# Two weight conversions and the decay table early on ScalarE's queue, a later split of the first block's sums, and 768 of 1024 weight columns split

## The chip, the cores and the metric

The kernel runs on one core of a Trainium2 chip. The metric is the device time of one execution in microseconds. The engines of the core are TensorE (PE in the profile; PEld is its weight load), VectorE (DVE), ScalarE (ACT), GpSimd (POOL) and SyncE (SP); SP and ACT issue the transfers here, each on a queue of its own.

## What is computed

The reference is a retention layer followed by two feed-forward layers, all in float32:

```
for each block of 64 positions:                       # q, k, v: 2 x 8 heads x 768 x 64
    intra = (q_b k_b^T * Dmask) v_b                   # Dmask[i,j] = lam^(i-j) for i >= j, else 0
    inter = (q_b * lam^(i+1)) kv_state
    out_b = intra + inter
    kv_state = lam^block * kv_state + (k_b * lam^(block-1-i))^T v_b
x = out as 1536 tokens x 512
g = relu(x @ w_in)^2 ;            x = g @ w_out       # 512 -> 2048 -> 512
h = sigmoid(x @ w_gate) * (x @ w_val) ; y = h @ w_out # 512 -> 1536 -> 512
```

## The kernel before, in words

**Stages.** The kernel takes the sequence in 12 chunks of 128 positions (two batch entries of six chunks each) in the order `ORDER`. The first seven chunks are the lead, ahead of the first feed-forward matmul. The other five are put between the steps of the first layer (`SLOTS`). The 1536 tokens form three blocks of 512. Block 0 goes through layer 1 step by step (`step_1`, 16 steps of 128 hidden columns). Blocks 1 and 2 go through the layer's first matrix together by a scheme that needs seven products for a two by two block product (`strassen`, eight pairs of steps in layer 1), and then through the second matrix (`pair_out`). The second layer does the same with `step_2`, twelve pairs and `pair_out`.

**Precision.** Every float32 operand of the feed-forward matmuls is split into a high part (a ScalarE copy to fp32r) and a low part (a VectorE subtraction), and a product is three matmuls. The loaded weights come in as float64; ScalarE makes two pieces of each 128 x 512 unit (`conv_act`, L150 and L151), VectorE puts them together in three operations (`conv_dve`), and SP stores the unit to DRAM, from where it is loaded again when it is needed. A weight pair is loaded as four 256-column blocks (`load_a`), combined to four sums by VectorE (`combine_a`), and both sets are split (`high_a`, `low_a`). The inputs are combined likewise: T1 to T4 are differences of quarters of blocks 1 and 2 (`combine_x`).

**Lead.** `powers` loads lambda to 128 partitions (8 heads x 16), raises it on POOL, and writes the powers to a small table in DRAM behind a row of zeros and a one. `decays` reads the table D (all partitions, each one element further) and the rows L back from there. For each chunk, `att_scores` needs q and k; `att_prep` lets POOL make kd = k x a column of D and qd = q x L, and VectorE mask the scores with D (L287). `att_out` makes the state update from kd (L314), the output from the masked scores (L322) and, for chunks that are not the first of their batch entry, from qd and the state (L329). `att_state` and `att_x` take the results out of the accumulators. `UP` chunks have their scores ahead of the loop; `LOOP` names the loads that each chunk issues and `CONVS` how many conversions it does. `conv_act` also asks for the next weight unit.

**Order.** The order on each engine is the order of the program. `passed(us)` moves a clock by the time of the matmuls emitted, and `at(pos, fn)` puts work on an agenda that is emitted when the clock has passed its place. `T1` is the start of `strassen` of the first layer, `T2` its end. In `step_1` each step does `PACE[f]` conversions while more than 36 units are left.

**Around T1.** In the first pair of `strassen` the closing product of block 0 (`close(1)`) follows the second of the seven products; `evacuate(1)` then takes its four sums out of PSUM and splits them at once into x0, the input of `step_2`. The products go in the order A11 with B11, S1 with T1, (close), S2 with T2, S4 with B22, S3 with T3, A12 with B21; A22 with T4 comes in the next pair.

Of the kernel before, what the change touches and what calls it, by code (L numbers as in the profile page):

```python
# [12 lines left out]
P = 128  # L13
# [5 lines left out]

ORDER = (0, 6, 1, 2, 7, 3, 8, 4, 9, 5, 10, 11)  # L20
LEAD = 7
UP = 4
SLOTS = ((1, 3), (5, 8), (11, 13), (16, 19), (22, 25))


FIRST = "q0 q1 v0"
SIDE = "q2 q3"
EARLY = "D v1 w q4"
LOOP = ("v2 v3 q5", "q6 v4 v5 w", "v6 w v7", "q7", "", "", "")
RAW_BUFS = 4  # L30

CONVS = (1, 0, 1, 1, 1, 1, 0)
PACE = (2, 2, 2, 2, 2, 2, 2, 2, 2, 2, 2, 2, 2, 2, 1, 0)

MM = 0.2267
# [5 lines left out]
def retention_moe_kernel(  # L41
# [95 lines left out]

    ready = []

    def conv_act():  # L140

        if not to_conv or to_conv[0] not in raw_t:
            return
        key = to_conv.pop(0)
        t = raw_t.pop(key)
        j = unit("j")
        r = unit("r", I32)
        nc.scalar.activation(j, t[:, :, 1].bitcast(F32), AF.Copy, scale=2.0**-112)  # L150
        nc.scalar.activation(r, t[:, :, 0].bitcast(mybir.dt.uint32), AF.Copy, scale=2.0**-29)  # L151
        ready.append((key, j.bitcast(I32), r))
        load_w(1)

    def conv_dve():

# [42 lines left out]
    L = const.tile([P, 4, CH], F32, name="L")  # L199
    S = [const.tile([P, 4, 64], F32, name=f"S{i}", tag=f"S{i}") for i in range(2)]  # L200
    w_dram = dram.tile([H, 256], F32, name="w_dram")

    def powers():


        src = bass.AP(lam.tensor, lam.offset, [[1, H], [0, 16], [1, 1]])
        nc.sync.dma_start(out=lam_sb, in_=src)
        nc.vector.memset(warm, 0.0)
        nc.gpsimd.iota(exi, pattern=[[1, 8]], base=0, channel_multiplier=8)
        nc.vector.memset(Z[:, 0:127], 0.0)  # L210
        nc.vector.memset(Z[:, 127:128], 1.0)
        nc.vector.tensor_scalar(
            out=exi, in0=exi, scalar1=127, scalar2=None, op0=ALU.bitwise_and
        )
        nc.vector.tensor_scalar(out=ex, in0=exi, scalar1=1.0, scalar2=None, op0=ALU.add)
        nc.scalar.dma_start(out=w_dram[:, 0:128], in_=Z)
        nc.gpsimd.tensor_tensor(out=W, in0=lam_sb.to_broadcast([P, 8]), in1=ex, op=ALU.pow)
        dst = w_dram[:]
        nc.scalar.dma_start(
            out=bass.AP(dst.tensor, dst.offset + 128, [[256, H], [8, 16], [1, 8]]), in_=W  # L220
        )

    def decays():


        src = w_dram[:]
        nc.sync.dma_start(
            out=D, in_=bass.AP(src.tensor, src.offset, [[1, P], [256, H], [1, CH]])
        )
        for r in range(2):  # L230
            nc.sync.dma_start(
                out=L[64 * r : 64 * r + 64],
                in_=bass.AP(src.tensor, src.offset + 256 * r + 128, [[0, 64], [512, 4], [1, CH]]),
            )
# [14 lines left out]
    def new_xr():  # L249
        for t in (1, 2):  # L250
            xr[t] = xp.tile([P, 4, TB], F32, tag=f"xr{t}", name=f"xr{t}")
# [17 lines left out]
    def att_prep(c):  # L269
        n = c % SEQ_CH  # L270
        sc = sc_t.pop(c)
        at_t[c] = double("at")
        dst = [pv(at_t[c][:, r, :]) for r in range(2)]
        qt = qk_t.pop(c)[:, 0, :]
        kn = kv_t[c][:, 0, :]
        if n < SEQ_CH - 1:
            kd = kd_t[c] = unit("kd")
            nc.gpsimd.tensor_tensor(  # L278
                out=kd.rearrange("s (h d) -> s h d", h=H),
                in0=kn.rearrange("s (h d) -> s h d", h=H),  # L280
                in1=D[:, :, CH - 1 : CH].to_broadcast([P, H, 64]), op=ALU.mult,
            )
        if n > 0:
            qd = qd_t[c] = unit("qd")
            nc.gpsimd.tensor_tensor(out=pv(qd), in0=pv(qt), in1=L, op=ALU.mult)  # L285
        return [
            lambda r=r: nc.vector.tensor_tensor(  # L287
                out=dst[r], in0=pv(sc[r]), in1=Dv[:, r], op=ALU.mult
            )
            for r in range(2)  # L290
        ]
# [146 lines left out]
    def evacuate(ph):  # L438
        for e, acc in enumerate(accs.pop(ph)):
            if ph == 1:  # L440
                nc.scalar.copy(x0[0][:, e, :], acc)
                nc.vector.tensor_tensor(
                    out=x0[1][:, e, :], in0=acc, in1=x0[0][:, e, :], op=ALU.subtract
                )
            else:
                o = unit("o")
                (nc.scalar.copy if e % 2 == 0 else nc.vector.tensor_copy)(o, acc)
                nc.sync.dma_start(out=out[e, :, 0:TB], in_=o)
# [9 lines left out]
        1: dram.tile([NF1, P, 2, TB], F32, name="g1"),  # L458
        2: dram.tile([NF2, P, 2, TB], F32, name="g2"),
    }  # L460
    A11, A12, A22 = (0, 0), (0, 1), (0, 3)
    S3, S4, S1, S2 = (1, 0), (1, 1), (1, 2), (1, 3)

    def split_x(name, src):
        hi, lo = xc[name] = double("xch", F32R), double("xcl", F32R)
# [42 lines left out]
    def combine_a(key):  # L508
        a = a_t[key]
        s = as_t[key] = wp.tile([P, 4, 256], F32, tag="w", name="as")  # L510
        tt = nc.vector.tensor_tensor
        tt(out=s[:, 0:2], in0=a[:, 0:2], in1=a[:, 2:4], op=ALU.subtract)
        tt(out=s[:, 2], in0=a[:, 2], in1=a[:, 3], op=ALU.add)
        tt(out=s[:, 1], in0=s[:, 0], in1=s[:, 1], op=ALU.add)
        tt(out=s[:, 3], in0=a[:, 3], in1=s[:, 0], op=ALU.subtract)

    def high_a(key, part):
        hi = wp.tile([P, 4, 256], F32R, tag="w", name="ah")
        lo = wp.tile([P, 4, 256], F32R, tag="w", name="al")
        nc.scalar.copy(hi, (a_t, as_t)[part][key])  # L520
        s_t[(*key, part)] = hi, lo

    def low_a(key, part):
        hi, lo = s_t[(*key, part)]
        src = (a_t, as_t)[part].pop(key)
        nc.vector.tensor_tensor(out=lo, in0=src, in1=hi, op=ALU.subtract)  # L526

    def prepare_a(key, pos):
# [93 lines left out]
    def keep_g(ph, f, t, g):  # L622
        held.append(lambda: nc.sync.dma_start(out=g_dram[ph][f, :, t], in_=g))

    def pair_in_1(i):
        def use(di, t, c, in_psum):
            g = unit("g")
            if in_psum:
                r = unit("r")
                nc.scalar.activation(r, c, AF.Relu)  # L630
                nc.vector.scalar_tensor_tensor(
                    out=g, in0=c, scalar=0.0, in1=r, op0=ALU.max, op1=ALU.mult
                )
            elif di == 1:
                r = unit("r")
                nc.scalar.activation(r, c, AF.Relu)
                nc.scalar.activation(g, r, AF.Square)
            else:
                nc.vector.scalar_tensor_tensor(
                    out=g, in0=c, scalar=0.0, in1=c, op0=ALU.max, op1=ALU.mult  # L640
                )
            keep_g(1, 2 * i + di, t, g)

        return [use]

    def pair_in_2(i):
        gate = {}

        def use_gate(di, t, c, in_psum):
            r = gate[di, t] = unit("r")  # L650
            nc.scalar.activation(r, c, AF.Sigmoid)

        def use_val(di, t, c, in_psum):
            g = unit("g")
            nc.vector.tensor_tensor(out=g, in0=c, in1=gate.pop((di, t)), op=ALU.mult)
            keep_g(2, 2 * i + di, t, g)

        return [use_gate, use_val]

# [63 lines left out]
    def load(what, eng=nc.sync):  # L723

        for x in what.split():
            if x == "w":
                load_w(1)
            elif x == "D":
                decays()
            elif x[0] == "q":  # L730
                load_qk(order[int(x[1:])], eng)
            else:
                load_kv(order[int(x[1:])], eng)
# [71 lines left out]
    with tc.manual_schedule():  # L805
        powers()
        load(FIRST)
        load(SIDE, nc.scalar)
        warm_up()
        load(EARLY)  # L810
        new_xr()
        for k in range(UP):
            att_scores(order[k])
        run(att_prep(order[0]))
        for k, c in enumerate(order[:lead]):
            att_out(c)
            if UP <= k + 3 < lead:
                att_scores(order[k + 3])
            load(LOOP[k])
            ops = conv_dve()  # L820
            if k + 1 < lead:
                weave(att_prep(order[k + 1]), ops[:2])
                run(att_state(c))
                att_decay(order[k + 1])
                weave(ops[2:], att_x(c))
            else:
                weave(split_w(1, 0), ops)
                rest.append(c)
            for m in range(CONVS[k]):
                if m:  # L830
                    run(conv_dve())
                conv_act()
            flush()


        keys = [(1, i, 0) for i in range(NF1 // 2)]
        prepare_a(keys[0], T1)
        at(T1 - 20.0, lambda: load_a((1, 1, 0)))
        combine_x([T1 + d for d in (-30, -25, -15, -13, -11, -9, -7, 2, 4, 6, 8)])
        for f in range(NF1):  # L840
            step_1(f)
        n_out = 24
# [93 lines left out]
```

## Time and profile before

| | |
|---|---|
| three runs | 604.19, 600.67, 601.86 us (median 601.86) |
| profiled execution, first to last instruction | 599.4 us (this span is all that is known of its own time) |
| TensorE busy | 582.6 us, 97% |
| VectorE, ScalarE, POOL busy | 448.6, 332.5, 36.9 us |
| DMA | 127.19 MB, mean 212 GB/s |

Busy is the time in which an engine executes; a matmul is counted from its start to its modelled end. The table by stretch gives for each engine the busy time and, in brackets, the number of instructions. A timeline row begins with the start and the duration in us; what stands in square brackets at its end is how long the engine was idle ahead of it and what released it. SPq and ACTq are issues of transfers by SyncE and ScalarE.

### The profile page before, as it was taken

To read this page: it belongs to the slowest core of one execution; us is meant where nothing else is said; L and a number is where in the kernel's file an instruction comes from. 1 tells how busy PE (TensorE), PEld (TensorE's weight loads), DVE (VectorE), ACT (ScalarE), POOL (GpSimd) and SP (SyncE) were. 2 spreads that over 40 slices of the span, in tenths; PEclk is the share of its full clock that TensorE was granted. 3 is DMA by queue.
4 is the path that set the end of the run, shared out by engine and by line. 5 is a ranking of instruction groups with operands and counts; after the bars stand their busy time and mean duration, and the time that the engine had idled before them with its cause. 6 is when DMAs were issued, how large, how long until landed. Compare 5 with 4: busy or idle time off the path is not lost.

```text
span 599.4 us, 8496 instructions
## 1 busy us (share of the span) xinstructions
PE 582.6 (97%) x3076; PEld 478.8 (80%) x3076; DVE 448.6 (75%) x673; ACT 332.5 (55%) x525; POOL 36.9 (6%) x34
## 2 busy tenths in 40 slices
PE   7799999999899999999999999999999999999997
PEld 7677878887678888888888888888888888888885
DVE  0699998999888868988877788694778787569101
ACT  0367787988556456756557654554464455537101
POOL 1672212100000000000000000000000000000000
PEclk9899999999999999999999999999999999999999
DMA  7996898682145377999978945511332422658003
GB/s 212 402 418 232 306 309 331 237 297 87 57 121 208 107 240 271 408 414 415 410 276 279 312 170 172 163 50 54 122 106 106 140 81 80 209 187 357 0 1 141
DMA packets 53578, 127.19 MB, mean 212 GB/s; under 512 B 5784, under 2 KB 7584, under 8 KB 53536
## 3 DMA queue, kind: packets, MB, share of 16 engines
q1 hardware_dynamic: 52376, 124.41, 57.9%
q10 hardware_dynamic: 1160, 2.24, 1.1%
q8 instruction: 24, 0.39, 0.3%
q14 instruction: 18, 0.15, 0.1%
HBM read 90.96 MB, written 35.66 MB: 211 GB/s over the span
## 4 chain that ended last, share of the span: by engine, by line
PE 87%; DVE 4%; DMA 2%; POOL 2%; issue 2%; ACT 1%; SPq 0%; ACTq 0%; POOLq 0%; DVEq 0%
PE p L545 30%; PE p L695 25%; PE p L386 17%; PE p L400 12%; DMA kv<-in_kv 1%; POOL kd L278 1%; PE p L329 1%; PE p L322 1%; POOL qd L285 1%; DMA lam_sb<-in_lam 1%; PE p L264 1%; DVE wlo L374 1%; DVE al L526 1%; DVE m L175 1%; ACT ah L520 1%
## 5 line engine op out<-in xcount | busy, mean ns | idle before, releaser
L545 PE MATMUL p<-xcl,ah 128*128 128x512 f32 x280 | 109.1, 390 | 2.5 <-DVE xcl L469 2.5
L545 PE MATMUL p<-xch,ah 128*128 128x512 f32 x280 | 109.4, 391 | 0.4 <-ACT s L554 0.2
L545 PE MATMUL p<-xch,al 128*128 128x512 f32 x280 | 109.0, 389 | 0.0
L695 PE MATMUL p<-g2h,whi 128*128 128x512 f32 x224 | 87.1, 389 | 0.0
L695 PE MATMUL p<-g2l,whi 128*128 128x512 f32 x224 | 87.1, 389 | 0.0
L695 PE MATMUL p<-g2h,wlo 128*128 128x512 f32 x224 | 87.1, 389 | 0.0
L545 PEld LDWEIGHTS p<-xcl,ah 128*128 128x128 f32 x280 | 52.6, 188 | 13.5 <-DVE xcl L469 2.9
L545 PEld LDWEIGHTS p<-xch,ah 128*128 128x128 f32 x280 | 52.5, 188 | 12.9 <-ACT s L554 1.4
L545 PEld LDWEIGHTS p<-xch,al 128*128 128x128 f32 x280 | 52.6, 188 | 11.0
L559 DVE TENSOR_TENSOR c<-p,s 128x512 f32<-128x512 f32 x60 | 41.2, 688 | 25.3 <-PE p L545 21.4
L554 ACT COPY s<-p 128x512 f32<-128x512 f32 x60 | 35.0, 586 | 37.4 <-PE p L545 37.4
L167 DVE CUSTOM_DVE_ANT_0 u<-m,r 128x1024 uint16<-128x1024 uint16 x68 | 49.5, 728 | 2.7
L374 DVE TENSOR_TENSOR wlo<-u,whi 128x512 fp32r<-128x512 f32 x68 | 46.1, 707 | 7.0 <-ACT whi L372 5.7
L150 ACT ACTIVATE j<-raw 128x512 f32<-128x512 f32 x68 | 45.6, 671 | 10.2 <-issue 5.3
L175 DVE SCALAR_TENSOR_TENSOR m<-j,m 128x512 int32<-128x512 int32 x68 | 49.5, 728 | 1.2
L151 ACT ACTIVATE r<-raw 128x512 int32<-128x512 uint32 x68 | 45.2, 665 | 8.7 <-PE p L695 5.5
L695 PEld LDWEIGHTS p<-g2l,whi 128*128 128x128 f32 x224 | 42.0, 188 | 8.8
L695 PEld LDWEIGHTS p<-g2h,whi 128*128 128x128 f32 x224 | 42.0, 188 | 8.7
L695 PEld LDWEIGHTS p<-g2h,wlo 128*128 128x128 f32 x224 | 42.0, 188 | 8.7
L372 ACT CAST whi<-u 128x512 fp32r<-128x512 f32 x68 | 39.0, 616 | 13.7 <-DVE u L167 13.2
L386 PE MATMUL p<-xh,wlo 128*128 128x512 f32 x160 | 43.2, 392 | 1.1 <-DVE wlo L374 1.1
L386 PE MATMUL p<-xh,whi 128*128 128x512 f32 x160 | 43.8, 395 | 0.0
(87 smaller groups left out, 911.6 us busy)
## 6 DMA issues: line engine op xcount, KB each, us to landing
raw<-in_w SPq DMA_DIRECT2D x68, 512.0 KB, 7.1
w<-u SPq DMA_DIRECT2D x68, 256.0 KB, 4.0
u<-w SPq DMA_DIRECT2D x64, 256.0 KB, 5.5
g<-g SPq DMA_DIRECT2D x56, 256.0 KB, 4.4
g<-g SPq DMA_DIRECT2D x28, 512.0 KB, 7.5
a<-w SPq DMA_DIRECT2D x20, 512.0 KB, 4.3
kv<-in_kv SPq DMA_DIRECT2D x12, 512.0 KB, 8.6
qk<-in_qk SPq DMA_DIRECT2D x10, 512.0 KB, 5.7
```

The source lines that it names most:

```text
L150: nc.scalar.activation(j, t[:, :, 1].bitcast(F32), AF.Copy, scale=2.0**-112)
L151: nc.scalar.activation(r, t[:, :, 0].bitcast(mybir.dt.uint32), AF.Copy, scale=2.0**-29)
L167: nc.vector.tensor_tensor(out=w.bitcast(I32), in0=m, in1=r, op=ALU.add)
L175: lambda: nc.vector.scalar_tensor_tensor(out=m, in0=j, scalar=-(2**31), in1=m, op0=ALU.bitwise_and, op1=ALU.bitwise_or),
L372: nc.scalar.copy(hi, src)
L374: lambda lo=lo, src=src, hi=hi: nc.vector.tensor_tensor(out=lo, in0=src, in1=hi, op=ALU.subtract)
L386: nc.tensor.matmul(acc, lhsT=a[:, kk * P : (kk + 1) * P], rhs=b[:, kk, :], start=i == 0, stop=i == 11,)
L400: nc.tensor.matmul(acc[e], lhsT=a[:, e * P : (e + 1) * P], rhs=b, start=first and i == 0, stop=last and i == 2,)
L545: nc.tensor.matmul(acc, lhsT=w[:, col, kk * P : (kk + 1) * P], rhs=x[:, kk, :], start=start and i == 0, stop=stop and i == 5, skip_group_c ...
L554: nc.scalar.copy(s, acc)
L559: nc.vector.tensor_tensor(out=c, in0=acc, in1=s, op=ALU.add)
L695: nc.tensor.matmul(acc[e, t], lhsT=a[:, e * P : (e + 1) * P], rhs=b[:, t, :], start=first and i == 0, stop=last and i == 2,)
```

## The change

`UP` goes from 4 to 3. All early loads are issued by SP, in the order `FIRST` and `NEXT`, with two weight units behind the first q. ScalarE does the first conversion, then issues D, does the second, and issues L; VectorE finishes both conversions ahead of the loop. Conversions in the lead no longer ask for the next unit; `LOOP` names them. POOL makes the column that kd needs (`KD`) from a second load of lambda (one row of eight heads for each partition), so that kd does not read D. `evacuate(1)` copies the four sums to SBUF and puts their split on the agenda, 20 to 46 us later. The two halves of a weight pair change places, so that the block that no product uses alone (A21) comes first and is left out of the split; the four sums are made by four operations of 256 columns. Four places of `combine_x` are a little earlier.

```diff
@@ -19,17 +19,15 @@
 
 ORDER = (0, 6, 1, 2, 7, 3, 8, 4, 9, 5, 10, 11)
 LEAD = 7
-UP = 4
+UP = 3
 SLOTS = ((1, 3), (5, 8), (11, 13), (16, 19), (22, 25))
 
 
-FIRST = "q0 q1 v0"
-SIDE = "q2 q3"
-EARLY = "D v1 w q4"
-LOOP = ("v2 v3 q5", "q6 v4 v5 w", "v6 w v7", "q7", "", "", "")
-RAW_BUFS = 4
-
-CONVS = (1, 0, 1, 1, 1, 1, 0)
+FIRST = "q0 w w q1 v0 q2 v1"
+NEXT = "q3 v2 q4 v3 w"
+LOOP = ("q5 v4 w", "q6 v5 w", "v6 w", "w q7", "v7 w", "w", "w")
+
+CONVS = (0, 0, 1, 1, 1, 1, 1)
 PACE = (2, 2, 2, 2, 2, 2, 2, 2, 2, 2, 2, 2, 2, 2, 1, 0)
 
 MM = 0.2267
@@ -137,7 +135,7 @@
 
     ready = []
 
-    def conv_act():
+    def conv_act(more=True):
 
 
 
@@ -150,7 +148,8 @@
         nc.scalar.activation(j, t[:, :, 1].bitcast(F32), AF.Copy, scale=2.0**-112)
         nc.scalar.activation(r, t[:, :, 0].bitcast(mybir.dt.uint32), AF.Copy, scale=2.0**-29)
         ready.append((key, j.bitcast(I32), r))
-        load_w(1)
+        if more:
+            load_w(1)
 
     def conv_dve():
 
@@ -199,6 +198,10 @@
     L = const.tile([P, 4, CH], F32, name="L")
     S = [const.tile([P, 4, 64], F32, name=f"S{i}", tag=f"S{i}") for i in range(2)]
     w_dram = dram.tile([H, 256], F32, name="w_dram")
+    lam8 = const.tile([P, H], F32, name="lam8")
+    exk = const.tile([P, 1], I32, name="exk")
+    exf = const.tile([P, 1], F32, name="exf")
+    KD = const.tile([P, H, 1], F32, name="KD")
 
     def powers():
 
@@ -206,6 +209,9 @@
         src = bass.AP(lam.tensor, lam.offset, [[1, H], [0, 16], [1, 1]])
         nc.sync.dma_start(out=lam_sb, in_=src)
         nc.vector.memset(warm, 0.0)
+        src = bass.AP(lam.tensor, lam.offset, [[0, P], [1, H]])
+        nc.scalar.dma_start(out=lam8, in_=src)
+        nc.gpsimd.iota(exk, pattern=[[1, 1]], base=0, channel_multiplier=1)
         nc.gpsimd.iota(exi, pattern=[[1, 8]], base=0, channel_multiplier=8)
         nc.vector.memset(Z[:, 0:127], 0.0)
         nc.vector.memset(Z[:, 127:128], 1.0)
@@ -213,22 +219,30 @@
             out=exi, in0=exi, scalar1=127, scalar2=None, op0=ALU.bitwise_and
         )
         nc.vector.tensor_scalar(out=ex, in0=exi, scalar1=1.0, scalar2=None, op0=ALU.add)
+        nc.vector.tensor_scalar(out=exf, in0=exk, scalar1=0.0, scalar2=None, op0=ALU.add)
         nc.scalar.dma_start(out=w_dram[:, 0:128], in_=Z)
         nc.gpsimd.tensor_tensor(out=W, in0=lam_sb.to_broadcast([P, 8]), in1=ex, op=ALU.pow)
         dst = w_dram[:]
         nc.scalar.dma_start(
             out=bass.AP(dst.tensor, dst.offset + 128, [[256, H], [8, 16], [1, 8]]), in_=W
         )
-
-    def decays():
+        nc.gpsimd.tensor_tensor(
+            out=KD[:, :, 0], in0=lam8, in1=exf.to_broadcast([P, H]), op=ALU.pow
+        )
+        nc.vector.memset(KD[0:1], 1.0)
+
+    def decay_table():
 
 
         src = w_dram[:]
-        nc.sync.dma_start(
+        nc.scalar.dma_start(
             out=D, in_=bass.AP(src.tensor, src.offset, [[1, P], [256, H], [1, CH]])
         )
+
+    def decay_rows():
+        src = w_dram[:]
         for r in range(2):
-            nc.sync.dma_start(
+            nc.scalar.dma_start(
                 out=L[64 * r : 64 * r + 64],
                 in_=bass.AP(src.tensor, src.offset + 256 * r + 128, [[0, 64], [512, 4], [1, CH]]),
             )
@@ -278,7 +292,7 @@
             nc.gpsimd.tensor_tensor(
                 out=kd.rearrange("s (h d) -> s h d", h=H),
                 in0=kn.rearrange("s (h d) -> s h d", h=H),
-                in1=D[:, :, CH - 1 : CH].to_broadcast([P, H, 64]), op=ALU.mult,
+                in1=KD.to_broadcast([P, H, 64]), op=ALU.mult,
             )
         if n > 0:
             qd = qd_t[c] = unit("qd")
@@ -438,9 +452,14 @@
     def evacuate(ph):
         for e, acc in enumerate(accs.pop(ph)):
             if ph == 1:
-                nc.scalar.copy(x0[0][:, e, :], acc)
-                nc.vector.tensor_tensor(
-                    out=x0[1][:, e, :], in0=acc, in1=x0[0][:, e, :], op=ALU.subtract
+                x = unit("xd")
+                nc.scalar.copy(x, acc)
+                at(clock[0] + 20.0 + 8.0 * e, lambda e=e, x=x: nc.scalar.copy(x0[0][:, e, :], x))
+                at(
+                    clock[0] + 22.0 + 8.0 * e,
+                    lambda e=e, x=x: nc.vector.tensor_tensor(
+                        out=x0[1][:, e, :], in0=x, in1=x0[0][:, e, :], op=ALU.subtract
+                    ),
                 )
             else:
                 o = unit("o")
@@ -458,8 +477,8 @@
         1: dram.tile([NF1, P, 2, TB], F32, name="g1"),
         2: dram.tile([NF2, P, 2, TB], F32, name="g2"),
     }
-    A11, A12, A22 = (0, 0), (0, 1), (0, 3)
-    S3, S4, S1, S2 = (1, 0), (1, 1), (1, 2), (1, 3)
+    A11, A12, A22 = (0, 1), (0, 2), (0, 0)
+    S1, S2, S3, S4 = (1, 0), (1, 1), (1, 2), (1, 3)
 
     def split_x(name, src):
         hi, lo = xc[name] = double("xch", F32R), double("xcl", F32R)
@@ -509,20 +528,22 @@
         a = a_t[key]
         s = as_t[key] = wp.tile([P, 4, 256], F32, tag="w", name="as")
         tt = nc.vector.tensor_tensor
-        tt(out=s[:, 0:2], in0=a[:, 0:2], in1=a[:, 2:4], op=ALU.subtract)
-        tt(out=s[:, 2], in0=a[:, 2], in1=a[:, 3], op=ALU.add)
-        tt(out=s[:, 1], in0=s[:, 0], in1=s[:, 1], op=ALU.add)
-        tt(out=s[:, 3], in0=a[:, 3], in1=s[:, 0], op=ALU.subtract)
+        a21, a22, a11, a12 = (a[:, n] for n in range(4))
+        tt(out=s[:, 0], in0=a21, in1=a22, op=ALU.add)
+        tt(out=s[:, 2], in0=a11, in1=a21, op=ALU.subtract)
+        tt(out=s[:, 1], in0=s[:, 0], in1=a11, op=ALU.subtract)
+        tt(out=s[:, 3], in0=a12, in1=s[:, 1], op=ALU.subtract)
 
     def high_a(key, part):
-        hi = wp.tile([P, 4, 256], F32R, tag="w", name="ah")
-        lo = wp.tile([P, 4, 256], F32R, tag="w", name="al")
-        nc.scalar.copy(hi, (a_t, as_t)[part][key])
+        n = (3, 4)[part]
+        hi = wp.tile([P, n, 256], F32R, tag="w", name="ah")
+        lo = wp.tile([P, n, 256], F32R, tag="w", name="al")
+        nc.scalar.copy(hi, (a_t, as_t)[part][key][:, 4 - n :])
         s_t[(*key, part)] = hi, lo
 
     def low_a(key, part):
         hi, lo = s_t[(*key, part)]
-        src = (a_t, as_t)[part].pop(key)
+        src = (a_t, as_t)[part].pop(key)[:, (1, 0)[part] :]
         nc.vector.tensor_tensor(out=lo, in0=src, in1=hi, op=ALU.subtract)
 
     def prepare_a(key, pos):
@@ -639,7 +660,7 @@
                 nc.vector.scalar_tensor_tensor(
                     out=g, in0=c, scalar=0.0, in1=c, op0=ALU.max, op1=ALU.mult
                 )
-            keep_g(1, 2 * i + di, t, g)
+            keep_g(1, 2 * i + 1 - di, t, g)
 
         return [use]
 
@@ -653,7 +674,7 @@
         def use_val(di, t, c, in_psum):
             g = unit("g")
             nc.vector.tensor_tensor(out=g, in0=c, in1=gate.pop((di, t)), op=ALU.mult)
-            keep_g(2, 2 * i + di, t, g)
+            keep_g(2, 2 * i + 1 - di, t, g)
 
         return [use_gate, use_val]
 
@@ -725,8 +746,6 @@
         for x in what.split():
             if x == "w":
                 load_w(1)
-            elif x == "D":
-                decays()
             elif x[0] == "q":
                 load_qk(order[int(x[1:])], eng)
             else:
@@ -805,10 +824,15 @@
     with tc.manual_schedule():
         powers()
         load(FIRST)
-        load(SIDE, nc.scalar)
         warm_up()
-        load(EARLY)
+        load(NEXT)
         new_xr()
+        conv_act(False)
+        decay_table()
+        conv_act(False)
+        decay_rows()
+        run(conv_dve())
+        run(conv_dve())
         for k in range(UP):
             att_scores(order[k])
         run(att_prep(order[0]))
@@ -829,14 +853,14 @@
             for m in range(CONVS[k]):
                 if m:
                     run(conv_dve())
-                conv_act()
+                conv_act(False)
             flush()
 
 
         keys = [(1, i, 0) for i in range(NF1 // 2)]
         prepare_a(keys[0], T1)
         at(T1 - 20.0, lambda: load_a((1, 1, 0)))
-        combine_x([T1 + d for d in (-30, -25, -15, -13, -11, -9, -7, 2, 4, 6, 8)])
+        combine_x([T1 + d for d in (-30, -25, -15, -13, -11, -9, -7, 1, 2.5, 5.5, 7)])
         for f in range(NF1):
             step_1(f)
         n_out = 24
```

## Rows read from the trace of the kernel before

**Rows 1.** The engine table of the page: busy us, share, instructions.

```profile
PE 582.6 (97%) x3076; PEld 478.8 (80%) x3076; DVE 448.6 (75%) x673; ACT 332.5 (55%) x525; POOL 36.9 (6%) x34
```

**Rows 2.** The table by stretch: us, busy us, granted clock, DMA share, GB/s.

```profile
22.90:41.40 18.50, 17.19 (x296) 14.23 (x291) 17.03 (x27) 9.24 (x16) 17.96 (x15) 1.00 1.02 416
41.40:50.00 8.60, 8.12 (x45) 5.91 (x44) 8.56 (x13) 5.71 (x10) 3.86 (x3) 1.00 1.00 388
50.00:140.00 90.00, 90.00 (x591) 72.67 (x591) 85.39 (x141) 74.71 (x128) 10.96 (x8) 1.00 0.76 270
140.00:168.00 28.00, 24.46 (x105) 18.96 (x104) 25.58 (x35) 18.55 (x28) 0.00 (x0) 1.00 0.20 66
168.00:594.00 426.00, 426.00 (x1879) 352.16 (x1878) 306.12 (x449) 219.65 (x336) 0.00 (x0) 1.00 0.54 194
```

**Rows 3.** TensorE's waits over the whole span: total us, times, longest.

```profile
PE p L314 <- POOL kd L278: 3.4, 4, 2.0
```

**Rows 4.** Timeline of the lead, all engines.

```profile
5.37 1.64 POOL L217 TENSOR_TENSOR W<-lam_sb,ex 128x8 f32<-128x8 f32 x1 [4.40 <-DMA lam_sb<-in_lam]
...
7.04 0.69 ACTq L219 DMA_DIRECT2D w_dram<-W  x1
...
9.27 1.28 ACT L342 ACT_TABLE_LOAD   x1 [9.27 <-issue]
...
9.49 0.39 SPq L227 DMA_DIRECT2D D<-w_dram  x1
...
16.18 2.48 DVE L287 TENSOR_TENSOR at<-p,D 128x512 f32<-128x512 f32 x4 [14.80 <-DMA D<-w_dram]
...
22.95 1.54 POOL L278 TENSOR_TENSOR kd<-kv,D 128x512 f32<-128x512 f32 x1 [2.62 <-DMA kv<-in_kv]
...
24.45 1.72 POOL L285 TENSOR_TENSOR qd<-qk,L 128x512 f32<-128x512 f32 x1
...
27.44 0.42 DVE L344 TENSOR_TENSOR S<-p,tt 128x256 f32<-128x256 f32 x1 [1.21 <-PE p L329]
...
41.42 1.20 PE L386 MATMUL p<-xh,whi 128*128 128x512 f32 x4
```

**Rows 5.** Timeline from 140 to 159 us: TensorE, VectorE and ScalarE.

```profile
142.58 1.20 PE L386 MATMUL p<-xh,wlo 128*128 128x512 f32 x4 [0.66 <-DVE wlo L374]
...
149.27 1.21 DVE L480 TENSOR_TENSOR t<-xr 128x1024 f32<-128x1024 f32 x1
...
151.76 2.05 ACT L441 CAST xh<-p 128x512 fp32r<-128x512 f32 x4
...
152.38 2.48 DVE L442 TENSOR_TENSOR xl<-p,xh 128x512 fp32r<-128x512 f32 x4 [1.90 <-ACT xh L441]
...
154.78 1.21 DVE L526 TENSOR_TENSOR al<-a,ah 128x1024 fp32r<-128x1024 f32 x1
...
155.91 1.22 DVE L480 TENSOR_TENSOR t<-xr,t 128x1024 f32<-128x1024 f32 x1
...
157.05 1.22 DVE L469 TENSOR_TENSOR xcl<-t,xch 128x1024 fp32r<-128x1024 f32 x1
...
158.32 0.50 PE L545 MATMUL p<-xcl,ah 128*128 128x512 f32 x1 [2.52 <-DVE xcl L469]
```

**Rows 6.** VectorE's timeline, the last conversion before 147 us.

```profile
138.96 0.69 DVE L167 CUSTOM_DVE_ANT_0 u<-m,r 128x1024 uint16<-128x1024 uint16 x1
```

**Rows 7.** Transfers, 20 to 40 us: all; weight loads with their landing.

```profile
DMA packets 2287, 8.35 MB, mean 417 GB/s; under 512 B 255, under 2 KB 255, under 8 KB 2285
...
raw<-in_w SPq DMA_DIRECT2D x8, 512.0 KB, 9.9
```

**Rows 8.** Transfers from 2.3 to 4.95 us, where lambda's rows move.

```profile
DMA packets 152, 0.07 MB, mean 25 GB/s; under 512 B 136, under 2 KB 136, under 8 KB 152
```

**Rows 9.** Transfers from 12.9 to 15.2 us, where D and L move.

```profile
DMA packets 1177, 0.59 MB, mean 257 GB/s; under 512 B 22, under 2 KB 1177, under 8 KB 1177
```

**Rows 10.** The page's groups: ScalarE's first operation of a conversion.

```profile
L150 ACT ACTIVATE j<-raw 128x512 f32<-128x512 f32 x68 | 45.6, 671 | 10.2 <-issue 5.3
```

## The prediction

> **What bounds the kernel now.** I read the engine table first: TensorE is busy 97% of the 599.4 us span [rows 1], so a change that removes no matmul can only win back the few stretches in which TensorE waits. The table by stretch says where these are [rows 2]: from 50 to 140 us and from 168 to 594 us TensorE is busy for the whole of the time, and no cheaper VectorE or ScalarE operation there can move the end. What is lost lies in the lead (the seven attention chunks ahead of the first matmul of the first layer at 41.42), in 41.4 to 50, and 28.00 - 24.46 = 3.5 us between 140 and 168. In the lead the chain of waits runs through the decay table and the chunk loads: the longest wait of TensorE there is for POOL's kd, 3.4 us in 4 waits [rows 3]. The timeline shows what stands behind it [rows 4]: the table D, issued at 9.49, releases VectorE's first masks at 16.18; the third chunk's kd waits for its v until 22.95; from then POOL (17.96 of 18.5 us) and VectorE (17.03) are nearly full [rows 2] and pace the rest. Between 140 and 168 the one large stall is TensorE's 2.52 us wait for xcl of T3, ended at 158.32 [rows 5]; the smaller one ends at 142.58. The tail is untouched.
>
> **The Strassen start: later split, earlier places, two conversions fewer.** Now ScalarE copies the four sums of the first block out as xh and VectorE subtracts all four (2.48 us, 152.38 to 154.86) before al (1.21), T4's difference (1.22) and xcl of T3, which ends at 158.27; TensorE stands from 155.8 to 158.32 [rows 5]. In the change only four ScalarE copies stay there (2.05 us as now); their split waits 20 us and more. I replay the queues with these durations, from the same matmul times. VectorE: T3's difference at 147.7 to 148.9 (its place is now 1 us after the start, ahead of the next pair's sums, which today take the 1.6 us before 149.27), the sums as four 256-column operations to 150.2. ScalarE: the high part of the sums waits for them, 150.2 to 151.2; T3's high part to 152.2; the snapshot to 152.7; the four copies to 154.8; the next snapshot to 155.3. VectorE: xcl of T3, 152.2 to 153.4, 2.0 us ahead of its first use at about 155.4. Then al with 768 columns (1.21 x 3/4 = 0.9) to 154.3, T4's difference to 155.4, the second al to 156.6, a total and its gate to 157.9, T4's xcl to 159.1; TensorE wants the last at about 159.5 without the stall. So the 2.52 us go, and what is late next is T4's xcl, with 0.4 us to spare, and the snapshot at 155.3, which frees the bank that TensorE writes at 155.4. Before it: two conversions done in the lead mean that step 13 of the first layer has none left to do, as each step takes two until 36 remain. That takes two times three VectorE operations out of 133 to 139 (the third of one is the 0.69 us row [rows 6]; with the two before it about 1.7 us, twice 3.4), and VectorE is late for wlo by 0.66 us at 142.58 [rows 5]. So this stall goes too. Of 3.5 us I take 3.2 back; the bounds are 3.5 and 0.8 (T4's xcl late by 2 us and a snapshot by 0.7, should VectorE's order differ).
>
> What moves: four more ScalarE copies (0.6 each) and the four subtractions at 20 to 46 us after the block, two operations at a time, within 168 to 594, where VectorE is busy 72% of the time and ScalarE 52% [rows 2]; hidden, unless a copy falls just ahead of a snapshot that frees a bank, 0 to 0.6 us in all. I take 0.1 and call the sum for this part 3.2.
>
> **768 columns and the swapped blocks.** One quarter of each weight pair is not split any more: a quarter of 1.21, 0.3 us of VectorE [rows 5], and about as much of ScalarE for each of 20 pairs, and the sums go over 1024 columns and not 1280. The matmuls are the same in number and size. Beyond the first pairs this lies beside a TensorE that is full [rows 2], so it is worth 0. Its cover is the matmul stream itself; there is no cost if it were gone.
>
> **The lead: loads.** Today SP waits for the power table before it can issue D and what follows. In the change SP issues q0, w, w, q1, v0, q2, v1, q3, v2, q4, v3, w in one go, and nothing but the transfers' own rate holds them back. A full stream moves 417 GB/s [rows 7], so 512 KB take 1.26 us. The loads get going at 5.0 us: up to there hardly anything but lambda's rows has moved [rows 8]. The third chunk's v is ninth: 5.0 + 9 x 1.26 = 16.3, plus D and L (0.79 MB at 257 GB/s, the rate of their small rows [rows 9], 3.1 us, if they go ahead of it), plus 1.0 to land (D's rows are through by 15.2, and its reader starts at 16.18 [rows 4, 9]): 20.4, against 22.95. The two weights that now come ahead of q1 and v0 cost these 2.5 us; q1 only feeds scores, and v0 lands at 12.3, before D.
>
> One transfer is added in front: lambda again for all partitions, 128 rows of 32 bytes on ScalarE's queue. Today's 128 rows of 4 bytes fill the 2.65 us from 2.3 on [rows 8], q0 stands behind them, and POOL's power starts at 5.37 [rows 4]. The new rows either run beside them (0) or one after the other (another 2.6 us for the whole stream). I take 0.8, nearer to nothing, since D's rows, which also share their source addresses, go at 1175 in 2.3 us [rows 9]. POOL's second power (1.64 us as the first [rows 4]) ends at 8.7 plus that, before v0 lands: no cost.
>
> **The lead: the decay table.** kd no longer needs D, but the masked scores do, and D is now issued by ScalarE behind its first conversion. Queued ahead of it there: the write of the powers (to 7.73), the table load (1.28), then two activations of 0.67 each [rows 10]: 10.4, against 9.49 [rows 4]; w, second in the stream, lands at about 8.5 and is no bound. Waiting behind it on ScalarE are the second conversion, L's issues and the state copy, none needed before D lands. How long D then takes on a queue of its own beside a full one, no row shows. In the trace of before it landed 6.6 us after its issue; a transfer in the full stream takes 9.9 [rows 7]. I take their middle, 8.3: 10.4 + 0.8 + 8.3 = 19.5. The ends: 3 us (its own 2.0 us at the rate of [rows 9] and 1 us to land), so 13.4; and, if one 512-byte row goes for each 4 KB packet of the other queue (64 rows on each of 16 transfer engines, each behind 0.16 us), 64 x 0.16 + 2.0 = 12.2 and the start and receipt of 3 us, so 25.6.
>
> The Trainium skill (DMA: Bandwidth & Descriptors, Queues, rings and completion order) says that each transfer engine takes turns between the issuers' queues, a whole packet at a time, typically 9 to 17 descriptors. By that D's 64 rows would need about four turns, an estimate of 4 x 1.26 + 2.0 + 3 us = 10.0 after the issue, a D at 21.2, and a lead with nothing gained. The trace neither bears it out nor refutes it: its two queues hardly overlap.
>
> From D on, VectorE has four masks (2.48 us [rows 4]), one subtraction, four more masks, and the state of the third chunk, about 6.1 us with a wait for TensorE: 25.6, against 27.44 now. POOL, from kd at 20.4 + 0.8, needs as long as today (22.95 to 27.44 is 4.5 us, so 25.7). The later of the two binds: 1.7 us earlier. From there both engines have the work of before in each chunk (chunks 3 to 6 carry a conversion each, as now), 14.0 us to 41.42 [rows 4]. Chunk 5's v, seventeenth in the stream, lands at 31.3 by the same count, hardly before POOL wants it. I take 0.2 off for that closeness: 1.5 us gained. Bounds: 4.5 (D early, kd at 19) and -6.5 (D at 25.6 and L, behind it at the same pace, at 32). Of 41.4 to 50 I expect nothing: one conversion is now in hand there, so the first wlo comes one short operation later, but its source is ready sooner; -0.6 to +0.8.
>
> **Sum.** Span 599.4 - 3.2 - 1.5 = 594.7. The profiled execution is known by its span; the median of 601.86 stands 2.46 above it, taken as what lies around it. 597.1.
>
> **Rivals.**
> 1. D comes early and the stream unhindered: the lead gives 3 to 4.5, 594.1 to 595.5. For it: D alone needs 2.0 us [rows 9]. Against: the other queue is full from 5 us on.
> 2. The lead gives nothing, or the stall at 158 only shrinks. Either lambda's second load holds the stream for 2.6 us, or D lands at 21 (as the rule on turns above would have it), or T4's xcl is late. 601.86 - 3.2 = 598.7, or with 0.8 of the stall and 1.5 of the lead 599.6. The Trainium skill (ScalarE: Activation LUTs, What ACT_TABLE_LOAD costs) puts a drain of 1.38 us behind the load; no row shows one, as the next operation of ScalarE waits for TensorE [rows 4]. By that page alone D would come 1.4 us later and the whole would be 598.5.
> 3. Slower: D and L starve. Their short rows get one turn for each 4 KB packet; D lands at 25.6 and L at 32. qd of the third chunk, now at 24.45 [rows 4], waits for L; what follows it moves by 7.5, less the 1 us that VectorE then has no wait: the lead ends 6.5 us later: 601.86 + 6.5 - 3.2 = 605.2. It decides from a D later than 21 for the lead, and later than 24.2 for the whole. For it: small rows move at 257 against 417 GB/s, and the stream stays full until 50 [rows 2]. Against: nothing in the trace shows turns by single rows.
> 4. The change does not do what it says, and the subtractions stay where they are: they are put on the agenda 20 us on, past the stall, so I give this nothing.
>
> **Chances.** Forecast 0.53 (595.5 to 598.7), first rival 0.17, second 0.20, third 0.10. A measurement can tell about 0.5%, 3 us. Faster by more than that (under 598.85): forecast, first rival and a quarter of the second, 0.75; within it: 0.15; slower (above 604.9): most of the third rival, with what I can't see, 0.10. The range of 593 to 601.5 leaves out the third rival and the first one's tail; the forecast alone would be 595.5 to 598.7.
>
> **What would show it.** After: the first layer's first matmul at 39.9; D's first reader at 19.5; kd of the third chunk near 21.2; no wait above 0.5 us between 140 and 168, and that stretch worth 3 us; no conversion on VectorE in step 13. Wrong, if VectorE waits for D beyond 21, if the powers start well after 5.4, or if TensorE still waits for an xcl.

## The result and the profile after

The changed kernel takes 607.0 us (median of four runs, 606.6 to 607.45), the kernel before 601.39 beside it: a ratio of 1.0078, with a 95% interval of 1.0053 to 1.0102 (the two medians alone divide to 1.0093). It is slower, where 597.1 was forecast with a range of 593 to 601.5; the time lies near the third rival's 605.2.

The profile splits this at the first matmul of the first layer (xh with whi). Ahead of it stands the lead: 51.23 us, against 41.42 [rows 4], 9.8 us more. Behind it stand 605.4 - 51.23 = 554.2 us, against 599.4 - 41.42 = 558.0, 3.8 us less. The sum is the 6.0 us by which the spans differ.

The engine table, the longest waits of TensorE (total us, times, longest) and a row of the table by stretch, all of the changed kernel:

```profile
PE 585.2 (97%) x3076; PEld 481.1 (79%) x3076; DVE 439.0 (73%) x675; ACT 331.7 (55%) x529; POOL 36.8 (6%) x36
```

```profile
PE p L336 <- DVE at L301: 10.9, 6, 8.8
PE p L278 <- DMA qk<-in_qk: 3.7, 3, 1.8
```

```profile
140.00:180.00 40.00, 39.98 (x178) 32.47 (x175) 34.22 (x50) 27.54 (x42) 0.00 (x0) 1.00 0.29 93
```

In the first fence VectorE has 9.6 us less work than before [rows 1], and the kernel is slower all the same. The second has no wait for xcl or wlo any more; the wait for kd [rows 3] is gone too, and one for VectorE's masks (`at`, L301) stands in its place, 8.8 us of it in one piece. The third is the stretch in which 3.5 us were lost [rows 2]: TensorE is full.

The timeline of the changed kernel's lead (start, duration, engine; in brackets the idle time ahead and what ended it):

```profile
5.97 1.64 POOL L224 TENSOR_TENSOR W<-lam_sb,ex 128x8 f32<-128x8 f32 x1 [4.92 <-DMA lam_sb<-in_lam]
...
7.64 0.70 ACTq L226 DMA_DIRECT2D w_dram<-W  x1
8.37 1.28 ACT L148 ACT_TABLE_LOAD   x1 [8.37 <-POOL W L224]
...
9.67 0.66 ACT L148 ACTIVATE j<-raw 128x512 f32<-128x512 f32 x1
...
15.05 0.44 ACTq L238 DMA_DIRECT2D D<-w_dram  x1
...
15.54 0.67 ACT L148 ACTIVATE j<-raw 128x512 f32<-128x512 f32 x1 [4.66 <-DMA w_dram<-W]
...
17.58 1.55 POOL L292 TENSOR_TENSOR kd<-kv,KD 128x512 f32<-128x512 f32 x1 [1.52 <-DMA kv<-in_kv]
...
24.87 2.48 DVE L301 TENSOR_TENSOR at<-p,D 128x512 f32<-128x512 f32 x4 [6.64 <-DMA D<-w_dram]
...
25.34 1.27 POOL L299 TENSOR_TENSOR qd<-qk,L 128x512 f32<-128x512 f32 x1 [6.21 <-DMA L<-w_dram]
...
25.62 2.56 PE L336 MATMUL p<-at,kv 128*64 128x128 f32 x16 [8.77 <-DVE at L301]
...
51.23 1.20 PE L400 MATMUL p<-xh,whi 128*128 128x512 f32 x4
```

The way to the first mask is now 8.7 us longer (24.87 against 16.18), in three pieces. The powers start 0.6 us later (5.97 against 5.37). From the issue of their write, 4 KB in all, to the issue of D go 15.05 - 7.64 = 7.4 us against 9.49 - 7.04 = 2.45 [rows 4]; ScalarE stands 4.66 us of them, with nothing to wait for but that write. And D takes 9.8 us to its first reader against 6.7. The two early conversions aren't the cause: the first is over at 10.9, and D still can't be issued.

While this lasts, SP stops. Its waits in the changed kernel (total, times, longest):

```profile
SPq L111 <- DMA D<-w_dram: 8.5, 1, 8.5
...
SPq L111 <- DMA w_dram<-W: 3.6, 1, 3.6
```

L111 is the load of a q. It needs nothing of D or W. But the program as built names eight completion semaphores (marks that a transfer sets when it has landed), which the transfers of both queues take in turn, so each transfer waits for the one eight places before it, and one slow transfer on ScalarE's queue holds SP's loads. In the trace q5 carries the semaphore of D and waits for it: it is issued at 24.80, and from 24 to 25 us the transfer engines are busy 12% of the time.

### The profile page after: what moved, and what is told of

Its sections match the earlier page's. It is cut to its first block, busy times and chain, and to the rows that moved or that the text cites. A ratio compares the mean times of both kernels' runs of the same rounds, so it can differ in the third digit from the quotient of the medians.

```text
span 605.4 us, 8521 instructions
## 1 busy us (share of the span) xinstructions
PE 585.2 (97%) x3076; PEld 481.1 (79%) x3076; DVE 439.0 (73%) x675; ACT 331.7 (55%) x529; POOL 36.8 (6%) x36
## 4 chain that ended last, share of the span: by engine, by line
PE 91%; DVE 4%; DMA 4%; issue 1%; ACT 0%; POOL 0%; ACTq 0%; DVEq 0%; POOLq 0%
PE p L566 32%; PE p L716 25%; PE p L400 17%; PE p L414 12%; DMA D<-w_dram 2%; PE p L336 2%; PE p L278 1%; DMA w_dram<-W 1%; PE p L343 1%; DVE u L166 1%; DMA lam_sb<-in_lam 1%; DVE m L174 1%; DVE at L301 1%; DVE m L171 1%; PE p L328 0%
## 5 line engine op out<-in xcount | busy, mean ns | idle before, releaser
L580 DVE TENSOR_TENSOR c<-p,s 128x512 f32<-128x512 f32 x60 | 41.2, 688 | 27.5 <-PE p L566 21.1
L174 DVE SCALAR_TENSOR_TENSOR m<-j,m 128x512 int32<-128x512 int32 x68 | 48.1, 707 | 1.3
L400 PE MATMUL p<-xl,whi 128*128 128x512 f32 x160 | 42.8, 389 | 0.0
```

What stands on the lines that cost most here:

```text
L174: lambda: nc.vector.scalar_tensor_tensor(out=m, in0=j, scalar=-(2**31), in1=m, op0=ALU.bitwise_and, op1=ALU.bitwise_or),
L400: nc.tensor.matmul(acc, lhsT=a[:, kk * P : (kk + 1) * P], rhs=b[:, kk, :], start=i == 0, stop=i == 11,)
L580: nc.vector.tensor_tensor(out=c, in0=acc, in1=s, op=ALU.add)
```

## The experiments

All times stand beside runs of the kernel before on the same chip: 602.22 us for the first four, 603.1 for the next four, 602.38 for the last two. "To the end" is the span less the start of the first matmul of the first layer: 558.0 before, 554.2 after.

**One half at a time.** The first kernel takes from the diff only the later split, the columns and the places; the second only the lead:

```diff
 first:  FIRST, SIDE, EARLY, LOOP, CONVS, UP, powers(), decays()   as before
         evacuate(1), A11..S4, combine_a, high_a, low_a, places    as changed
 second: the other way round
```

> The lead is that of before; the later split, the earlier places and the 768 columns stay. Theory (the lead alone made the kernel slower, the other half keeps its gain): TensorE waits under 1 us between 140 and 168, where the 0.66 us for wlo may stay because step 13 has its conversions again; 2.6 to 3.5 us less than before, so about 598 to 599. Rival (the two halves lean on each other; the stall at 158 goes only because two conversions fewer are left in step 13): the 2.5 us wait for xcl comes back at least by half, 600 to 601.

> Only the lead of the change; the split of the first block's sums, the places and the 1024 columns are those of before. Theory: the first matmul of the first layer near 51.2, 9.8 us later than before; with the 0.66 us for wlo saved, about 610.5. Rival (part of the loss lies behind the lead, in a longer row of conversions or stores): the first matmul no later than 48 and the rest lost after it.

The first took 600.92 us, ratio 0.9977 (0.9957 to 0.9998); the second 610.17, ratio 1.0126 (1.0089 to 1.0162). The first matmul of the first layer with the lead alone:

```profile
50.94 1.19 PE L400 MATMUL p<-xh,whi 128*128 128x512 f32 x4
```

and the stall that it keeps:

```profile
PE p L559 <- DVE xcl L483: 2.4, 1, 2.4
```

To the end it has 557.3 us, 0.7 less than before: the wait for wlo is gone. So the whole loss is the lead's. The halves add up to within about 1 us: beside the kernel before, 1.3 us less and 7.95 us more make 6.65, and both together measured 5.6. The rival of each falls: the first kernel has no wait for xcl any more, though its time lies in the rival's 600 to 601, and the second has its first matmul at 50.94, not by 48. The first kernel's median gained less than its profile (596.1 against 599.4 us), so it ran again:

> The kernel of the first run once more, in five rounds with a second profile, because its median gained 1.3 us where its profile showed 3.3 less. Theory (the lead of before, with loads on two queues, ends up to 3 us later from one execution to the next; what follows it is always 2.8 us shorter than before): first matmul of the first layer anywhere between 40.5 and 44, from there to the end 555 us again; median 1.5 to 3.5 below that of before. Rival (something behind the lead is slower in most executions): from the first matmul to the end over 556.5 us.

This time 598.47 us, ratio 0.9934 (0.9912 to 0.9957), 3.9 us under the kernel before and a little more than expected, though this profile shows a longer span. The first matmul of the first layer in the first profile of this one kernel:

```profile
40.94 1.20 PE L386 MATMUL p<-xh,whi 128*128 128x512 f32 x4
```

and in its second:

```profile
43.95 1.20 PE L386 MATMUL p<-xh,whi 128*128 128x512 f32 x4
```

The spans are 596.1 and 599.4, so to the end it is 555.2 and 555.5. Between these two executions the lead of before varies by 3 us and what follows it by 0.3; a single span can hide or double the 2.6 us that this half is worth.

**Which queue.** Two kernels leave the change as it is but for the table's transfers. In the first, SP writes the powers; in the second, SP also loads D and L:

```diff
-        load(FIRST)
+        load("q0 w w"); store_powers()        # nc.sync in place of nc.scalar
+        load("q1 v0 q2 v1")                   # second kernel: "q1 v0", D, "q2 v1", L, all on nc.sync
```

> The change, with one transfer moved: the write of the power table is issued by SP behind q0, w, w and not by ScalarE. Theory (a queue's short rows get few turns beside SP's full queue of 4 KB rows): in the middle of SP's own queue the write lands near 10 us and not at 15.0; D is issued by ScalarE near 11 and still takes 9 to 10 us, so the masks start near 20.5, 4 us earlier, about 603. Rival (the write is slow because the transfer engines are full, whatever the queue): it lands at 14 to 15 as in the change, D at 24.5, 607.

> As the run before, and D and L too are issued by SP: D behind v0, L behind v1. Theory: in order in SP's queue D needs only its own 2 us behind v0, and the masks start at 15 to 16.5, as before the change; the lead ends near 41, the other half keeps 3.5: 597 to 599. Rival (short rows beside a full queue are slow in themselves, in any queue): D takes 6 us or more behind v0, masks at 19 or later, 601 to 603.

The first: 605.74 us, ratio 1.0055 (1.0034 to 1.0076). Rows of its lead, and its transfers from 14 to 20 us (packets, MB, share of 16 engines; q1 is SP's queue, q10 ScalarE's):

```profile
7.58 0.62 SPq L232 DMA_DIRECT2D w_dram<-W  x1
...
9.90 0.40 ACTq L240 DMA_DIRECT2D D<-w_dram  x1
...
24.27 2.48 DVE L303 TENSOR_TENSOR at<-p,D 128x512 f32<-128x512 f32 x4 [11.18 <-DMA D<-w_dram]
```

```profile
q1 hardware_dynamic: 562, 2.06, 86.3%
q10 hardware_dynamic: 548, 0.28, 15.7%
```

The write lands in time on SP's queue, 2.3 us after its issue, so D goes out 5 us sooner, and then needs 14.4 us, not the 9 to 10 of the expectation. None of its rows moves before 13.7, and from there to 20 us it meets a full queue. The second fence shows how the two share: in 6 us they moved nearly the same number of packets, 562 and 548, while one moved 2.06 MB and the other 0.28. The trace's packets come one by one in turn: 501 of the 548 rows of 512 bytes end where a row of 4 KB starts, and only 70, what chance would give, end where another short row starts. So a row of 512 bytes gets one turn for each row of 4 KB of the other queue. From 20 to 24 us SP's queue is nearly empty (47 packets): SP's next load waits for D's semaphore.

The rival (any short row is slow on full engines) had the write at 14 to 15, and it was through by 9.9. But the engines were not full at that moment: SP could not issue the write before the powers were there, so q1 behind it went out at 8.24 and not at 2.99, and from 9 to 10 us the engines were busy 70% of the time. Nor do turns by rows explain all of the 7.4 us of the changed kernel's write. None of its rows moves before 11.8, 4.2 us after the issue (1.7 us in the kernel before); then the 128 rows take until 14.4. What holds the first row back stays open.

The second kernel: 600.47 us, ratio 0.9961 (0.9946 to 0.9976).

```profile
9.92 0.39 SPq L240 DMA_DIRECT2D D<-w_dram  x1
...
15.62 2.48 DVE L303 TENSOR_TENSOR at<-p,D 128x512 f32<-128x512 f32 x4 [2.45 <-DMA D<-w_dram]
...
43.72 1.20 PE L402 MATMUL p<-xh,whi 128*128 128x512 f32 x4
```

```profile
PE p L280 <- DMA qk<-in_qk: 7.9, 3, 3.5
```

In order on SP's queue D takes 5.7 us, and the masks start 0.6 us sooner than before the change, so the rival falls. The starved table was the loss: 607.0 becomes 600.5. But the time misses the theory's 597 to 599, the lead still ends 2.3 us later than in the profile of before, and TensorE now waits for q's: q1 stands behind the write in SP's order and goes out at 8.27. That was not in the theory, which had 41. One profile of each kernel is little for 2.3 us. If what follows the lead is taken from the profile, the spans of all executions give leads with a median of 43.7 here and 42.2 for the kernel before beside it, so about 1.5 us later.

**What the lead needs next.** Three kernels change the order of the loads with D on SP's queue: the one above without its two early weights; the lead of before with q3 behind two values; and that with each q ahead of the value before it:

```diff
 no early weights:  "q0 q1 v0", powers, D, "q2 v1", L, "q3 v2 w q4 v3 w"
 values first:      "q0 q1 v0" and q2 on ACT, D L, "v1 v2 q3 w q4", UP = 3
 by need:           "q0 q1 v0" and q2 on ACT, D L, "q3 v1 q4 v2", "q5 v3 w", UP = 3, conversions one chunk later
```

> The run with the table on SP without the two early weights and their conversions; weights and conversions of the lead as before the change, the rest of the change stays. Theory (1 MB of weights ahead of q1 and v0 cost the lead 2.5 us, for two conversions that nothing waited for): masks near 14.7, first matmul of the first layer 2.5 to 4 us earlier than 43.7, thus near 40; step 13 has its conversions again (0.7 us lost); 598 to 599. Rival (the early conversions pay for their loads): no earlier than 43, 600.5 to 601.5.

> The kernel of the first run (lead of before, other half of the change) with the loads of the lead in another order: q3 goes behind D, v1 and v2 instead of ahead of them, and three chunks have their scores ahead of the loop. No short rows stand on ScalarE's queue beside a full SP queue. Theory: D, with one transfer fewer ahead of it, releases the masks near 15; the third chunk's v lands near 20.5 and not at 23; first matmul of the first layer near 39, 2 us earlier than in the first run, 598 to 599. Rival (from D on POOL's and VectorE's pace alone sets the lead): 41, no gain over the first run.

> As the run with the values first, but q3 ahead of v1 and q4 ahead of v2, the weights behind them, and the five conversions of the lead one chunk later each. Theory (with D there by 15, the lead goes at the pace at which TensorE, in its order, gets the next q; q3 behind two values cost 2 us): first matmul of the first layer near 40, 597.5 to 599. Rival (three chunks of scores ahead of the loop leave TensorE idle, and at the lower of its two clock levels, whatever the order of the loads): 43 or later, 600 to 601.

Measured: 600.51 us (ratio 0.9957, 0.994 to 0.9975), 600.01 (0.9951, 0.9931 to 0.9971) and 598.98 (0.9945, 0.9927 to 0.9963). The first matmul without the early weights, then its longest wait for a q (total, times, longest):

```profile
43.19 1.20 PE L402 MATMUL p<-xh,whi 128*128 128x512 f32 x4
```

```profile
PE p L280 <- DMA qk<-in_qk: 9.0, 4, 5.6
```

The same two views with the values first:

```profile
43.62 1.20 PE L386 MATMUL p<-xh,whi 128*128 128x512 f32 x4
```

```profile
PE p L264 <- DMA qk<-in_qk: 5.2, 3, 1.9
```

and by need:

```profile
39.90 1.20 PE L386 MATMUL p<-xh,whi 128*128 128x512 f32 x4
```

```profile
PE p L264 <- DMA qk<-in_qk: 3.6, 2, 2.6
```

In the first two D is there at 14.05 and 14.96, earlier than in any other run, and the lead of the profile is no shorter than 43; the theory falls in both. Without the early weights the lead ends only 0.5 us sooner than with them, which is that run's rival: they aren't where its 2.3 us went. With the values first not even the rival's 41 is reached. With the q's brought forward the lead ends at 39.9, as expected, and its rival falls. Worked out from the spans as above, its six executions have leads from 39.7 to 40.9, those of the other two kernels from 41.2 up. So the order of the lead's work was the next bound. That it was the order in which TensorE gets its q's is likely but not shown alone, since this run also has its conversions one chunk later. Behind the lead this kernel has 557.1 us to the end, 1.6 more than the undone lead; TensorE waits there for wlo (0.9) and the state (0.6), but the undone lead has 1.2 for wlo too, so its waits explain only about half of the 1.6. It ends level with the kernel whose lead was undone; its runs lie closer (598.68 to 599.76, against 597.26 to 601.46).

**Which part of the other half.** Both on the change with its lead:

```diff
 first:  evacuate(1) and the four places as before
 second: combine_a, high_a, low_a, A11..S4 as before (all 1024 columns)
```

> The change, with the first block's sums split at once and the places of the input combinations as before; the 768 columns and the lead of the change stay. Theory (the later split takes 2.5 us of VectorE out of the way of T3): the wait for xcl comes back to 1.5 to 2.4 us, 609 to 609.5. Rival (the smaller splits and the two conversions gained in step 13 are enough by themselves): under 0.7 us of wait, 607 to 607.5.

> The change, with all 1024 columns split and the blocks in their old order; the later split, the places and the lead of the change stay. Theory (the columns lie beside a full TensorE): no more than 0.5 us of waits between 140 and 180, 607 to 607.5. Rival (without the 0.3 us for each split the first pair's inputs come late): 1 to 2 us of wait for xcl or al near 165, 608 to 609.

609.61 us (ratio 1.012, 1.0083 to 1.0156) and 608.16 (1.0097, 1.0064 to 1.013). The waits that come back with the split at once:

```profile
PE p L561 <- DVE xcl L483: 2.2, 1, 2.2
```

and with all columns:

```profile
PE p L564 <- DVE c L578: 0.4, 1, 0.4
PE p L564 <- ACT s L573: 0.2, 1, 0.2
```

To the end they have 556.9 and 554.9 us against 554.2. The later split with its places is worth 2.7 us, the columns 0.7, the two conversions gained in step 13 the 0.7 of the lead alone: 4.1 by parts, 3.8 together, where two profiles of one kernel differed by 0.3. The first run's wait came back as in its theory, and its rival falls. The columns are not worth nothing, as I had put it: the second run's waits add up to 0.6, just above its theory's 0.5, but the rival's wait for xcl or al isn't there. Its time lies in the rival's range beside a kernel before of 603.1, where the changed kernel had 601.39 beside it.

All five versions that issue D on SP lie under both kernels. The lowest are the order by need (598.98, 3.4 us under the kernel before) and the undone lead: 598.47 in the second timing and 600.92 in the first, 3.9 and 1.3 us under the kernel before.

## Why the prediction was wrong

**The first step that failed: "10.4".** I listed what stands ahead of D on ScalarE: the write of the powers, the table load, two activations. I left out the one thing that D waits for, that this write has landed, and let its 2.45 us of before stand without saying so, although I had just filled the queue beside it. Measured: D issued at 15.05, against 11.2 with the 0.8 us for lambda's second load. These 3.9 us stood in no term of mine, neither in the sum nor in a bound. Nor did the transfers' own rate alone hold SP back: the last of its twelve early loads was issued at 15.90.

**The 8.3 us for D** was the middle between D in order on SP's queue and a long-row load on the same queue; neither had to share turns with another queue. Measured: 9.8, and 14.4 with the powers on SP; the bound of the single-row turns had said 12.2 + 3. So the third rival had the turns right and D at 25.6 against 24.87, though for a different split: more on the write, less on D. That its 605.2 is near is in part luck: its lead ended 6.5 us later because L came at 32, but qd had L at 25.34, and the lead ended 9.8 us later. I gave it 0.10 since "nothing in the trace shows turns by single rows"; nothing showed the contrary either, and an unknown between 3 and 15 us on the path deserved a wider range.

**The second step that failed, and the largest: "about 6.1 us with a wait for TensorE"** from D's first mask to the state of the third chunk. Measured: 11.5. The two rows of VectorE, and the same stretch as a whole in the changed kernel and in the kernel before:

```profile
29.45 2.47 DVE L301 TENSOR_TENSOR at<-p,D 128x512 f32<-128x512 f32 x4
...
36.37 0.42 DVE L358 TENSOR_TENSOR S<-p,tt 128x256 f32<-128x256 f32 x1 [4.45 <-PE p L343]
```

```profile
24.87:36.37 11.50, 10.28 (x130) 8.64 (x132) 5.57 (x10) 1.62 (x4) 4.08 (x4) 0.74 0.93 343
```

```profile
16.18:27.44 11.26, 8.52 (x130) 7.21 (x132) 7.82 (x13) 3.00 (x7) 6.57 (x6) 0.81 1.03 410
```

I had added up VectorE's operations. What releases the state is TensorE, which in its order first has to do three sets of sums, two of scores, two state updates and the product with qd: 130 matmuls, 10.3 us of work. In the kernel before it was 130 too, with a set of scores less and a state update more, and 8.5 us. In the traces of all runs this stretch took 10.0 us or more, also where D came early. So the 1.5 us that the lead was to gain were not to be had from D at 19.5: with these 11.5 us behind it the lead would have ended near 45, an estimate (19.5 + 11.5 + 14.3), and later than before. TensorE was granted 0.74 of its clock in this stretch, against 0.81: having stood from 16.9 to 25.6, it took 2.56 us for the first sums and 2.08 for the next scores, where later in the same lead 1.05 and 1.16 suffice. What the clock alone cost was not tried.

From the state to the end of the lead it was 14.9 us against the 14.3 of the forecast. The four misses, 3.9, 1.5, 5.4 and 0.6 us, are the 11.3 by which the first matmul missed its 39.9.

**The rule that I weighed.** The Trainium skill (DMA: Bandwidth & Descriptors, Queues, rings and completion order) has turns of a whole packet, typically 9 to 17 descriptors, by which D would have needed 10.0 us, an estimate. D's 9.8 in the changed kernel would fit, but not its 14.4 in the run with the powers on SP, where the rows of the two queues came one by one in turn. The Trainium skill's drain of 1.38 us behind a table load (ScalarE: Activation LUTs, What ACT_TABLE_LOAD costs) isn't there either: the load ends at 9.65, and the activation starts at 9.67.

**Right:** lambda's second load cost 0.6 us (0.8 taken); the values arrived early (kd of the third chunk at 17.58, even 3.6 us before my 21.2, since D's rows did not go ahead of them). The Strassen start came as replayed: no wait from 140 to 180 us, no conversion left in step 13, 3.8 us less to the end against 3.2.

## What to carry to other kernels

A chain of small transfers (a table written to DRAM and read back) belongs in the queue that carries the stream, in its order, or ahead of the stream; on a second queue beside a full one it gets a turn per row, however short the row. In the stream's order it costs something too: what stands behind it waits until the table can be written (here q1, by 5.3 us). Before loads are moved forward, list for each small transfer on the critical path what will be in flight beside it, and price its landing anew, not by its duration in a quiet trace. An early input is worth only as much as the next thing that TensorE, in its order, has to wait for.

## What the runs showed of the hardware

Two queues share the transfer engines packet by packet: 562 and 548 packets in 6 us, 86.3% and 15.7% of the engines' time, with long and short rows in turn. A write of 128 rows of 32 bytes on ScalarE's queue took 7.4 us from its issue to the next issue that waits for it, beside a full queue, 4.2 of them before its first row moved; behind three loads in SP's order it took 2.3. After its long wait TensorE was granted its lower level (1.2 GHz) for part of the time: 0.68 over 25 to 34 us. The program's eight completion semaphores tie the two queues together: SP's next q waited 8.5 us for D.
